# Another order of issue for a gated delta-rule kernel with a dense layer behind it

## The chip, the cores and the metric

The kernel runs on one core of one Trainium2 chip. The metric is the device time of one execution in microseconds, the median over runs. Engines are named as in the profile: PE is TensorE (matmuls; PEld its weight loads), DVE is VectorE, ACT is ScalarE, POOL is GpSimd, SP is SyncE, which here only issues DMAs.

## The reference

A gated delta-rule attention over 4 batches, 8 heads, 768 steps and a head size of 48, then a dense layer with softplus on its 3072 rows of 384:

```python
for t in range(S):                       # _attn_ref
    kt, vt, bt = k_n[:, :, t], v[:, :, t], beta[:, :, t, None]
    readout = einsum('bhd,bhde->bhe', q[:, :, t], state)
    y[:, :, t] = g[:, :, t] * readout
    v_old = einsum('bhde,bhd->bhe', state, kt)
    state = state + bt * einsum('bhd,bhe->bhde', kt, vt - v_old)
...
h = x @ w_in                             # _moe_ref: 384 -> 2048 -> 384
return (softplus(h) @ w_out).astype(float32)
```

`k_n` is k divided by its norm. Step t reads the state that the steps before it wrote.

## The kernel before

The 768 steps are cut into 12 chunks of 64 (`c`), worked on in pairs (`cc`). All 32 batch-heads of a chunk go together. Within a chunk the recurrence is solved as a triangular system, so that the state passes only from chunk to chunk. The work is a list of 1168 *steps*, each with a number, a kind, the engines that it may run on and the steps that it depends on. These functions add them:

- `load`, `load_q`: DMAs of k, q, v and g, one chunk in two halves, issued by SP (two of k by ACT); the weights `w_in` and `w_out` come in quarters, issued by POOL.
- `norms` and `front`, for a chunk: squares and sums of k (ksq, red), the root (pow on POOL, L541), k times its inverse norm (kmul, L303), transposes (trs, L321 and L364) and their copies (kev), and the gram matrices (L405, L406, L438, L475, L476) with their copies (kkc) and masks.
- `inverse`, for a pair of chunks: prep (L592) and 15 serial steps of two small operations (L602, L609) on POOL, for the first pair on DVE; then the matmul steps xmm (L665), tmm (L686, L692) and zmm (L718, L721).
- `chain`, for a chunk, the recurrence: ks and qs (L759), w (L793), umm (L802, L806), zu (L827), smm (L847), s (L862), ymm (L877), y (L892), and the transposes ytr (L911).
- `dense`, for one or two chunks: g1 (L941, h = x @ w_in, three matmuls 512 wide or six 256 wide a step), softplus on ACT (L953), g2 (L968, o = ga @ w_out, four matmuls 384 wide a step), the copy of o and the store.

A g1 or g2 step is few large matmuls on the whole array. The steps of `inverse`, `chain` and the gram matrices are 16 to 68 matmuls on parts of 32 to 64 rows. Every matmul has its own weight load, so that TensorE runs 6112 of each, 12,232 instructions with a few of the frame, with no loop: the program is one straight list.

Nothing plans at run time. The order is a table, `_ORDER` (L1022), of words such as `P665`: a letter for the engine (P TensorE, D DVE, A ACT, G POOL, S SP) and the number of the step. `Program.emit` goes through it once:

```python
for word in table.split():
    en, no = word[0], int(word[1:])
    it = self.items[no]
    ...
    for b in it.bufs:
        if b.ap is None:
            b.slot = b.ring.free.pop(0)
    it.fn(en)
```

The words of one engine, taken out of the table, are the order in which that engine works, and it works strictly in that order. A step that needs what another engine made waits on a semaphore. Buffers come from rings (4 of k, 3 of q, 4 of v, 3 of g, 5 PSUM banks `d` for the small work, 2 `h`, 1 `o`); the table also decides who gets which slot and so which step must wait until a slot is free.

Of the kernel before, what the change touches and what calls it, by code (L numbers as in the profile page):

```python
# [1019 lines left out]


_ORDER = """  # L1022
S0 D226 D152 A1 D111 P114 D110 P112 D115 P124 A9 G227 A104 D105 A113 P121 S8 A106 D131 P134 S26
S3 S27 A130 S19 P132 A135 P144 D107 S18 A123 A108 D126 A125 D133 P141 D109 A145 A146 D150 D153
S25 G212 A122 S17 S2 S10 S33 G196 P197 S11 S42 S16 S41 D142 A143 D151 S5 D154 D155 D156 D157
D158 D159 D160 D161 D162 D163 A198 S24 S7 A116 A117 P118 A119 S34 A120 P127 S32 S35 S43 S4 D164
D165 D166 D167 D168 D169 D170 G171 S13 D129 A187 A137 D172 A136 S40 P213 P138 D188 A547 G173
D174 A140 A139 P147 D148 A189 D190 S12 S6 D548 D549 P175 A177 P176 A178 A259 D260 D128 P179 A181
A554 P180 A182 D298 G96 A261 D262 G97 P183 A184 P555 A556 D214 G98 G191 D192 P550 A551 D193 P557
P552 A558 P565 A553 P563 G99 D566 D564 D284 P194 A195 S14 S15 G209 P567 D568 P569 D570 P210 A211  # L1030
D149 P832 A833 P559 D571 P560 D562 P199 A200 A202 D203 D201 P838 A839 D561 P215 A216 D217 P220
A223 A221 P836 A837 D222 G263 D224 D264 P204 A207 A205 D206 P834 A835 G100 D219 D218 P285 G101
G268 P269 A270 P840 D225 P572 P579 D573 P844 A286 A845 D580 G102 G265 P266 D267 P575 A576 D208
P185 A186 P582 D583 P271 A272 D273 P574 P581 P584 D585 P577 A841 A274 P846 D275 G281 P282 P592
D593 A578 P590 A283 P848 D591 P287 D291 D289 A847 G228 G229 G230 G103 P292 D296 D295 D288 D290
P594 A595 S49 P842 A843 P849 G231 P868 A869 G232 G233 D293 G234 G235 G236 G237 G238 G239 G240
G241 S51 P866 A867 P276 D277 D279 D280 D297 P587 P586 D588 D278 P870 A871 D589 G242 G243 G244
G245 D246 P860 A861 P850 P851 A852 P862 A863 D247 P864 A865 S48 A331 P854 P855 P856 P857 A858
S20 S57 P249 P250 A251 D248 P596 P598 P603 D332 D294 S56 A333 D334 P253 P252 P876 P877 A254 S21
D604 D597 P255 S50 P606 A607 P599 P257 P605 D256 P608 A600 P601 A602 G299 G300 G301 G302 G303  # L1040
S23 S29 D340 D609 P872 A873 P611 P610 D612 D613 P614 G335 A258 P874 A875 D336 P341 A342 P627 S28
D628 P620 S58 D621 G304 G353 S22 D615 P878 P879 A880 P623 D624 P630 A631 P616 D617 P629 P622
P625 D626 P632 A633 P354 A355 P638 S31 S30 D639 P640 D641 P635 P634 D636 D637 S59 A356 P882 P618
G337 P338 D339 P642 D643 P357 G305 G306 G307 G308 P883 G309 S64 S65 A403 D404 P348 D350 A619
P898 P890 A358 P364 D367 D366 S67 A349 G310 D352 D368 A351 S66 G412 P359 D361 D363 D362 A899
A891 S73 S72 A405 P918 A919 P900 A901 G311 G312 G313 G314 D406 G315 G316 D317 D318 P884 P902
A903 P892 A893 D319 P885 A365 A360 P910 A911 P908 A909 D320 P343 A346 S90 A344 D369 S881 G370
G371 D345 P321 P322 A323 S74 P896 A897 D886 P888 A889 P325 P324 D326 S37 P651 S36 D652 P644 D645
P646 D347 S81 S80 A475 D476 S83 P894 A895 P912 A913 P413 A414 P906 S39 P329 D330 A907 S75 P647
G372 G373 A648 G374 G375 P327 D328 P654 P916 A917 P904 D655 A905 D428 P653 P656 A657 P649 G407  # L1050
D408 S44 G409 D650 G376 S89 S88 S46 S82 A484 S887 S53 A477 G377 P429 P914 A915 G378 G379 P658
S38 S47 P659 S853 P920 G380 P921 D430 P922 D661 P923 P664 A924 D478 D660 P675 D665 S45 P668 S69
P926 P927 P928 P929 D669 D676 P678 D930 S931 A679 G381 P671 D672 G425 P662 D663 P677 P680 S61
A681 G479 P670 S62 S54 P673 A674 P932 G382 G383 G384 G385 G386 P666 D667 P426 D427 P933 P410
A411 P686 D687 P688 P934 P935 A936 G387 D689 P690 D691 S70 P420 D422 P415 A416 A418 S63 D419
P938 D417 D421 P960 A961 P966 A967 D423 P436 P431 D439 D435 A432 A434 D437 G388 D441 P948 A949
P958 A959 S60 P939 P950 D514 D438 A951 S52 D389 D433 S68 D390 S859 S91 P964 A965 D480 G391 D392
P940 P968 S77 A969 D424 G442 P962 A963 P682 G443 G444 P683 D684 G445 S55 G446 D685 P393 P394
A395 P944 A945 P952 A953 P396 P397 A398 P692 D693 P699 P954 A955 A500 P946 A947 P941 A942 S943
D700 P399 P702 P695 D400 A696 D703 P970 A971 P974 G447 S937 G448 G449 G450 G451 G452 G453 G454  # L1060
G455 A975 G456 G457 G458 G459 G460 P701 P704 P694 P697 D705 G497 P956 A957 P972 A973 D698 D440
D461 D462 D463 D464 P976 P977 P978 P979 A980 P707 P706 D708 D709 P712 D713 P982 P983 P984 P985
A986 S987 P723 D724 P710 P716 D717 P401 A402 P465 P726 D727 P719 A720 S981 D711 P466 A467 P725
P728 A729 P718 P721 D481 S93 S78 P714 D715 P988 A722 S71 P734 D735 P736 D737 P730 P731 D732 P482
S79 S85 P989 S95 A483 P485 D486 P738 D733 P498 D499 P990 P991 A739 D992 S993 P1004 A1005 P501
D502 P1028 A1029 P1022 P994 A1023 P503 A504 S84 D507 D505 P492 D493 D494 D496 A506 D495 P1012
A1013 P995 P1018 A1019 S94 P1008 A1009 P508 D512 A509 A511 P487 D491 D489 A488 A490 D513 P469
P468 A470 P1020 D510 A1021 P996 P1010 P740 P747 A1011 D741 P471 G515 G516 G517 G518 G519 G520
S76 A472 D748 P473 A474 P743 P750 D751 A744 P1006 A1007 P1000 A1001 G521 G522 G523 P749 P742
P752 A753 P745 A746 P997 D998 P1002 A1003 P1026 A1027 S999 P760 D761 P758 D759 P754 P755 D756  # L1070
P1024 A1025 S87 G524 G525 S86 P1016 A1017 D757 P762 D763 P1014 A1015 P1030 A1031 P1032 P1033
P1034 P1035 D1036 G526 G527 G528 G529 G530 G531 P771 G532 A533 D534 S925 D772 P764 P773 D765
P1038 P1039 P1040 P1041 D1042 S1043 P767 D768 P774 P538 A775 P766 P769 D770 P776 A777 P537 D539
P782 D783 P784 P778 P779 P1044 P1045 D785 P786 D787 P1046 P1047 A1048 S1049 P1058 A1059 P1076
A1077 P1050 P1060 A1061 P1070 A1071 G535 D536 P540 S92 P541 A542 D781 D780 P788 P795 P1068 P1062
D796 A1063 A1069 P1051 P1052 P1078 A1079 P1064 A1065 P798 A799 D789 P543 A544 P791 P1080 A1081
P1072 A1073 D792 P790 P793 A794 P797 P800 A801 P1086 A1087 P806 P802 P808 P803 P1056 D807 D805
P1053 A1057 D809 D804 P1082 A1083 P810 P1066 D1054 A1067 P1074 A1075 D811 P1088 S1037 S1055
P1084 P1089 P1090 A1085 P1091 A1092 P1124 A1125 P1118 A1119 P1100 P1101 P1102 P1103 P819 D1104
S1105 D820 P812 D813 P821 P1094 P1095 P1096 P1097 P1126 D1098 S1099 P822 A823 P545 P815 A546  # L1080
P1106 D816 A1127 P1112 A1113 P1107 P1114 A1115 P1108 P1109 A1110 P824 D825 P814 P817 A818 P1116
A1117 P1122 A1123 P828 P826 P1128 D829 P1120 D827 A1121 P830 P1129 P1130 S1093 P1131 A1132 S1133
D831 P1148 A1149 S1111 P1144 A1145 P1134 P1135 P1146 A1147 P1140 A1141 P1136 P1142 A1143 P1150
A1151 P1137 D1138 S1139 P1154 P1152 A1155 A1153 P1162 P1163 P1164 P1165 A1166 S1167 P1156 P1157
P1158 P1159 A1160 S1161
"""

# [28 lines left out]
```

## Time and profile before

| | us |
|---|---|
| median of 3 runs | 302.21 |
| lowest and highest | 299.0, 303.22 |
| the profiled execution | 303.66 |
| its span, first to last instruction | 301.7 |

The profile is of one execution. "Busy" of an engine counts its instructions; that of PE is modelled from starts. A wait is written `who <- whom`; "issue" stands for a wait with no cause in the records. Kinds of DMA queues: hardware_dynamic and software_dynamic carry data, "instruction" carries the engines' programs. PEclk is the granted clock of TensorE in tenths, or as a share of 1. The mean granted clock of this execution is 0.920.

### The profile page before, as it was taken

The page shows a single profiled execution, that of the slowest core. Times are in us where ns is not written, and L with a number is a line of the kernel's source. Part 1 is how long each engine was busy: PE and PEld are TensorE (multiplying, and loading weights), DVE is VectorE, ACT ScalarE, POOL GpSimd, SP SyncE. Part 2 cuts the span into 40 slices and gives each one's busy share as a digit, 9 for nine tenths or more (in the row PEclk, how much of TensorE's full clock was granted, in tenths as well). Part 3 has the DMA queues.
Part 4 walks back from the last instruction along what each step waited for, and adds up shares of the span by engine and source line. Part 5 has one row for each costly group of instructions (what it writes and reads, how often), then busy time and mean ns, then how long its engine had stood idle before and what let it go on. Part 6 is the DMA issues. An engine that isn't in the chain of part 4 may idle for free.

```text
span 301.7 us, 13385 instructions
## 1 busy us (share of the span) xinstructions
PE 236.7 (78%) x6112; PEld 161.7 (54%) x6112; DVE 141.0 (47%) x307; ACT 131.7 (44%) x239; POOL 119.7 (40%) x217
## 2 busy tenths in 40 slices
PE   1353239869949976989996996998996999999960
PEld 1233137656737833566653566764564556667730
DVE  7689447824824775374680453553433324112000
ACT  3546245743524764562463523265520355334510
POOL 7204809986361882749868500006820000000000
PEclk9999999977978999799997897798997899999995
DMA  8999998999501099530683012841031110011111
GB/s 126 201 179 186 186 182 141 191 202 161 109 4 30 25 168 163 128 83 8 129 148 69 13 43 65 140 93 31 20 88 32 33 50 9 22 45 39 39 50 42
DMA packets 85480, 27.69 MB, mean 92 GB/s; under 512 B 75568, under 2 KB 85424, under 8 KB 85424
## 3 DMA queue, kind: packets, MB, share of 16 engines
q1 hardware_dynamic: 79376, 23.21, 42.2%
q0 software_dynamic: 3968, 3.25, 7.0%
q8 instruction: 47, 0.77, 1.2%
q10 hardware_dynamic: 2080, 0.39, 0.9%
q14 instruction: 9, 0.07, 0.1%
HBM read 25.26 MB, written 4.72 MB: 99 GB/s over the span
## 4 chain that ended last, share of the span: by engine, by line
PE 70%; DMA 10%; issue 9%; SPq 2%; POOL 2%; ACT 2%; DVE 1%; POOLq 0%; ACTq 0%; DVEq 0%
PE h L941 23%; PE o L968 22%; DMA kf<-in_k_dram 5%; PE d L759 4%; DMA beta_l<-in_beta_dram 3%; PE d L877 2%; PE d L827 2%; DMA out_dram<-osb 2%; PE d L665 2%; PE d L847 2%; PE d L692 2%; PE d L321 2%; PE d L911 2%; PE d L475 2%; PE d L721 1%
## 5 line engine op out<-in xcount | busy, mean ns | idle before, releaser
L941 PE MATMUL h<-xt,w_in 128*128 128x512 f16 (+1 forms) x384 | 78.2, 344 | 1.9 <-ACT ga L953 1.9
L968 PE MATMUL o<-w_out,ga 128*128 128x384 f16 x384 | 75.1, 341 | 0.7 <-ACT osb L200 0.6
L953 ACT ACTIVATE ga<-h 128x512 f16<-128x512 f32 x96 | 57.0, 597 | 37.4 <-PE h L941 35.0
L968 PEld LDWEIGHTS <-ga 128*128 128x128 f16 x384 | 37.6, 102 | 26.6 <-issue 4.6
L941 PEld LDWEIGHTS <-w_in 128*128 128x128 f16 x384 | 36.4, 101 | 24.6 <-issue 5.4
L609 POOL TENSOR_TENSOR tt<-tt,tmp 128x30 f32<-128x30 f32 (+7 forms) x75 | 27.7, 369 | 5.9
L541 POOL TENSOR_TENSOR nv<-nv,half_c 128x32 f32<-128x32 f32 x5 | 27.2, 5449 | 6.6 <-DVE nv L524 6.6
L602 POOL TENSOR_TENSOR tmp<-nn,tt 128x30 f32<-128x30 f32 (+7 forms) x75 | 26.5, 353 | 5.4
L200 ACT ACTIVATE u<-d 128x384 f16<-128x384 f32 x30 | 14.3, 490 | 26.3 <-PE d L806 14.6
L592 POOL TENSOR_TENSOR nn<-ln,beta_l 128x256 f32<-128x256 f16 x10 | 6.0, 619 | 42.9 <-DVE ln L574 42.9
L200 ACT ACTIVATE kqt<-d 128x1024 f16<-128x1024 f16 (+1 forms) x18 | 15.5, 877 | 16.2 <-PE d L321 12.2
L303 POOL TENSOR_TENSOR kn<-kf,nv 128x768 f16<-128x768 f32 x8 | 12.5, 1573 | 19.6 <-DVE nv L547 14.5
L200 ACT ACTIVATE osb<-o 128x384 f32<-128x384 f32 x14 | 6.9, 490 | 29.6 <-PE o L968 24.7
L493 DVE TENSOR_TENSOR mt<-d,mask 128x256 f16<-128x256 f32 x40 | 15.4, 411 | 8.8 <-ACT kk L200 5.4
L892 DVE TENSOR_TENSOR yg<-d,gf 128x384 f16<-128x384 f32 x24 | 12.7, 552 | 14.2 <-PE d L877 14.2
L202 DVE COPY osb<-o 128x384 f32<-128x384 f32 x10 | 5.5, 554 | 28.2 <-PE o L968 28.2
L793 DVE TENSOR_TENSOR w<-vf,d 128x384 f16<-128x384 f32 x22 | 11.1, 547 | 15.4 <-PE d L759 15.4
L759 PE MATMUL d<-s,kqt 48*64 48x48 f16 x704 | 16.2, 195 | 2.1 <-issue 2.1
L665 PE MATMUL d<-tn,kk 16*32 16x16 f16 x768 | 8.6, 171 | 11.8 <-issue 10.6
L202 DVE CAST u<-d 128x384 f16<-128x384 f32 x18 | 9.9, 554 | 16.4 <-PE d L806 8.9
L759 PEld LDWEIGHTS <-kqt 48*64 48x64 f16 x704 | 13.4, 115 | 6.3 <-issue 5.9
L524 DVE TENSOR_REDUCE nv<-ksq 128x16 f32<-128x768 f32 x12 | 11.3, 942 | 10.1 <-ACT ksq L520 10.1
(104 smaller groups left out, 361.7 us busy)
## 6 DMA issues: line engine op xcount, KB each, us to landing
qf<-in_q_dram SPq DMA_DIRECT2D x24, 192.0 KB
vf<-in_v_dram SPq DMA_DIRECT2D x24, 192.0 KB
gf<-in_g_dram SPq DMA_DIRECT2D x24, 192.0 KB
out_dram<-osb SPq DMA_DIRECT2D x24, 192.0 KB
kf<-in_k_dram SPq DMA_DIRECT2D x22, 192.0 KB
w_in<-in_moe_w_in_dram POOLq DMA_DIRECT2D x4, 384.0 KB, 9.0
w_out<-in_moe_w_out_dram POOLq DMA_DIRECT2D x4, 384.0 KB, 8.4
kf<-in_k_dram ACTq DMA_DIRECT2D x2, 192.0 KB
```

What stands on the lines that cost most here:

```text
L200: nc.scalar.activation(o, x, AF.Copy, scale=float(sign))
L202: ENG[en].tensor_copy(o, x)
L493: nc.vector.tensor_tensor(mt[c][m].ap[:, NP * p : NP * p + NP], gb[m].ap.rearrange("p (n b) -> p n b", n=NP)[:, :, C:], mask[:, None, :].b ...
L541: lambda en: nc.gpsimd.tensor_tensor(nv.ap, nv.ap, half_c, ALU.pow),
L602: eng.tensor_tensor(t, nn.ap[:, :, j + 1 :, j : j + 1].broadcast_to([P, 2, n, w]), tt.ap[:, :, j : j + 1, :w].broadcast_to([P, 2, n, w]), ...
L609: eng.tensor_tensor(rows, rows, t, ALU.add)
L665: nc.tensor.matmul(uv(xp.ap)[QUAD[qd], u], kk.ap[r, 0, u, :], tn.ap[r, u, :])
L759: nc.tensor.matmul(hd(o.ap)[HALF[r], NP * p + i], kq_of(c)[FEAT[m], 8 * p + 2 * i + r, off : off + C], s0[r].ap[FEAT[m], NP * p + i], **st ...
L892: lambda en, m=m: nc.vector.tensor_tensor(heads(yg.ap, m), hd(yp[m].ap), heads(gf.ap, m), ALU.mult),
L941: nc.tensor.matmul(hp.ap[:, n * b : n * b + n], w_in[:, j, f * P : (f + 1) * P], xt.ap[:, j, t0 : t0 + n], start=(j == 0), stop=(j == 2),)
L953: lambda en, hp=hp, o=gb: nc.scalar.activation(o.ap, hp.ap, AF.Softplus),
L968: nc.tensor.matmul(op.ap[:, :DM], b.ap[:, col + c0 : col + c0 + 128], w_out[:, f, :], start=(f == 0), stop=(f == NF - 1),)
```

## The change

Only the table `_ORDER` is another one. The steps, their matmuls, their tiles, the rings, and everything outside the table are unchanged. Its author searched the order with a model in which TensorE fetches its instructions in lines of 256. The two tables have the same 1168 numbers; 105 of them carry another engine letter (kinds kkc, u1, o, kev, xt, kmul, u2, xs, z and some others), all among D, A and G. Of the 431 words for TensorE, 23 stand at the same place among TensorE's words as before. The start, a middle piece and the end:

```diff
 _ORDER = """
-S0 D226 D152 A1 D111 P114 D110 P112 D115 P124 A9 G227 A104 D105 A113 P121 S8 A106 D131 P134 S26
-S3 S27 A130 S19 P132 A135 P144 D107 S18 A123 A108 D126 A125 D133 P141 D109 A145 A146 D150 D153
+D226 S0 D152 A1 D111 D110 P114 P112 A9 A104 A115 P124 D105 S8 A130 D113 P121 D131 P134 A106 D125
+D126 P132 A133 P141 D107 A108 D109 D150 A135 P144 S18 A123 A122 A142 A145 D153 S11 A137 D143
...
-A223 A221 P836 A837 D222 G263 D224 D264 P204 A207 A205 D206 P834 A835 G100 D219 D218 P285 G101
-G268 P269 A270 P840 D225 P572 P579 D573 P844 A286 A845 D580 G102 G265 P266 D267 P575 A576 D208
-P185 A186 P582 D583 P271 A272 D273 P574 P581 P584 D585 P577 A841 A274 P846 D275 G281 P282 P592
+D264 D281 P215 D217 S14 A216 P220 A223 D224 D222 P579 D580 A218 A221 D225 S15 S35 S34 P842 A843
+D219 P285 A286 P572 D573 P582 D583 P282 A283 P834 P147 D149 A839 P575 A576 P581 P584 D585 A835
+G99 P846 A847 P574 P577 A578 D148 G100 D265 P592 D593 P844 P590 A845 D591 P287 A288 G102 S49
...
-A1151 P1137 D1138 S1139 P1154 P1152 A1155 A1153 P1162 P1163 P1164 P1165 A1166 S1167 P1156 P1157
-P1158 P1159 A1160 S1161
+P1140 A1141 P1137 D1138 S1139 P1146 A1147 P1150 A1151 P1156 P1157 P1158 P1159 A1160 S1161 P1162
+P1163 P1164 P1165 A1166 S1167
 """
```

Numbers under 96 are loads, 96 to 103 the weights, 104 to 546 `norms`, `front` and `inverse`, 548 to 831 `chain` and 832 to 1167 `dense`. In the old table stretches of P words with numbers under 832 alternate with stretches of P words from 832 up; in the new one both kinds alternate more often.

More of the change, by code (lines that the diff above doesn't have):

```diff
@@ L1022 @@
 _ORDER = """
-S0 D226 D152 A1 D111 P114 D110 P112 D115 P124 A9 G227 A104 D105 A113 P121 S8 A106 D131 P134 S26
-S3 S27 A130 S19 P132 A135 P144 D107 S18 A123 A108 D126 A125 D133 P141 D109 A145 A146 D150 D153
[L1025 to L1028, printed above, removed]
@@ L1029 @@
-A554 P180 A182 D298 G96 A261 D262 G97 P183 A184 P555 A556 D214 G98 G191 D192 P550 A551 D193 P557
-P552 A558 P565 A553 P563 G99 D566 D564 D284 P194 A195 S14 S15 G209 P567 D568 P569 D570 P210 A211
-D149 P832 A833 P559 D571 P560 D562 P199 A200 A202 D203 D201 P838 A839 D561 P215 A216 D217 P220
-A223 A221 P836 A837 D222 G263 D224 D264 P204 A207 A205 D206 P834 A835 G100 D219 D218 P285 G101
-G268 P269 A270 P840 D225 P572 P579 D573 P844 A286 A845 D580 G102 G265 P266 D267 P575 A576 D208
-P185 A186 P582 D583 P271 A272 D273 P574 P581 P584 D585 P577 A841 A274 P846 D275 G281 P282 P592
@@ L1035 @@
[L1035 to L1082, printed above, removed]
@@ L1083 @@
-D831 P1148 A1149 S1111 P1144 A1145 P1134 P1135 P1146 A1147 P1140 A1141 P1136 P1142 A1143 P1150
-A1151 P1137 D1138 S1139 P1154 P1152 A1155 A1153 P1162 P1163 P1164 P1165 A1166 S1167 P1156 P1157
-P1158 P1159 A1160 S1161
+D226 S0 D152 A1 D111 D110 P114 P112 A9 A104 A115 P124 D105 S8 A130 D113 P121 D131 P134 A106 D125
+D126 P132 A133 P141 D107 A108 D109 D150 A135 P144 S18 A123 A122 A142 A145 D153 S11 A137 D143
+D146 D151 D154 D155 D156 D157 D158 D159 D160 S25 D161 D162 A547 D163 D164 S12 D165 D166 D167
@@ new lines @@
+D168 S17 S3 A117 S2 A116 P118 A119 A120 P127 D169 D170 D171 G173 S16 A187 D172 P175 D188 A177
+D174 P179 S24 S19 S10 S4 A189 S5 D548 P176 A549 D554 A181 D190 D129 S13 P550 S40 S33 P183 D128
+S32 A259 D260 A136 A551 P555 D556 A184 P552 D178 D571 S6 S41 A261 S7 P557 G97 A553 P563 D564
+A558 P565 G98 G196 P197 D566 P569 G191 D192 D570 P567 A568 D262 D193 P138 D140 S26 D139 A198
+P180 P840 P194 S27 D195 A182 S42 S43 D284 A841 P185 A212 P836 A186 P204 D206 D208 A837 G96 A205
+P560 A207 P559 D561 D562 G209 P213 A214 P199 D203 D201 A202 P210 A211 P838 P832 A200 A833 G263
@@ new lines @@
+D264 D281 P215 D217 S14 A216 P220 A223 D224 D222 P579 D580 A218 A221 D225 S15 S35 S34 P842 A843
+D219 P285 A286 P572 D573 P582 D583 P282 A283 P834 P147 D149 A839 P575 A576 P581 P584 D585 A835
+G99 P846 A847 P574 P577 A578 D148 G100 D265 P592 D593 P844 P590 A845 D591 P287 A288 G102 S49
+A290 G227 P292 P594 A293 G268 S48 D291 D294 D595 A295 P848 A331 P266 P586 P587 D588 D267 D589
+P860 A861 P870 A871 P269 A270 P862 A863 G101 P866 A867 D289 P276 A279 G103 P271 A272 G228 A274
+D332 G229 G230 G231 G232 G233 G234 G235 G236 G237 G238 G239 G240 G241 D296 G242 P864 G243 D277
@@ new lines @@
+S57 D275 A865 D280 G244 D245 G247 P849 P850 P851 D246 P250 P249 P874 A852 D297 D278 S56 P854
+A333 D273 A251 D334 A875 G298 G299 G300 G301 D248 P868 P872 A869 A873 S65 S50 P253 P252 A254
+P855 G302 G303 P856 P857 P603 S64 A403 D404 S20 P596 A858 S21 P876 D604 P606 G335 P255 D597 P599
+A600 P877 P878 A607 D256 S75 S51 P598 P601 A602 D340 D336 D353 P605 P608 A609 G304 G305 P879
+A880 P610 P611 D612 D613 P616 S58 P614 P354 A355 P882 P257 A258 S28 S59 D356 S22 P341 P357 G306
+S23 D617 D615 P618 A342 G307 A358 P622 D337 P627 P620 P883 S72 S29 D619 D628 P630 D621 P359 P623
@@ new lines @@
+D631 D361 S73 A405 D406 D363 S74 P884 A624 S31 A360 P625 G308 G309 S30 A362 G310 G311 P629 P632
+A633 G312 G313 G314 G315 G316 D317 D318 S81 P885 P640 D641 A626 P638 D639 P338 D339 G428 P429
+A430 P635 P634 D637 D636 P642 A643 P343 D345 G319 A344 P348 D351 D346 D352 A349 P902 A903 S68
+P364 A365 D366 D367 S80 D369 P888 A889 P908 A909 D368 G407 D408 D347 P322 D442 A475 P894 A895
+P904 A905 P321 A323 D476 P651 P644 P916 A917 D320 P910 A911 G370 G425 P426 S36 P896 P325 A897
+S45 S89 S88 A477 S37 D645 D652 D427 P324 A326 P912 A913 P906 D478 A907 P431 D433 S853 P890 A891
@@ new lines @@
+P918 A919 P647 D350 D435 D434 P654 A655 P327 A328 P900 A901 P898 A899 P646 S66 S39 D648 P649
+D650 P892 S44 S67 A412 P914 A893 D432 P653 P656 A657 P662 D886 G371 S881 S38 D663 P329 A915 D330
+P658 P659 D661 D660 P664 D665 G372 D409 P413 A414 P920 P921 P922 P923 D924 P436 A437 A439 D438
+D440 P675 G373 D676 G374 P668 D669 P926 S859 S82 G375 P927 S52 G479 D480 P410 S887 A411 P666
+D667 G376 G377 P678 A679 P671 G378 G379 G380 G381 S83 D672 P928 P929 S84 S71 D930 P677 P680 A681
+P670 P673 A674 S53 S46 P938 P939 S47 P686 D687 P688 D689 P940 P941 G382 D942 G383 G384 P690 A691
@@ new lines @@
+P420 A421 D423 P415 A416 D417 S91 G385 G386 G387 G388 G389 D390 G443 G391 P932 S70 D422 P933
+P958 A959 P948 A949 D418 D441 P393 D419 P394 D395 P683 P682 D685 P946 A947 P954 A955 G497 P934
+P966 A967 D392 P962 D514 G515 A963 S90 A500 P498 P970 P974 A975 D684 D481 P699 P692 P397 P396
+D484 A971 D700 D693 D398 P964 A965 P944 S925 S931 P501 A945 A502 D424 P956 A957 P399 A400 P401
+S55 P702 A703 D499 G444 G445 G446 G447 G448 G449 G450 G451 G452 G453 G454 G455 G456 G457 G458
+G459 G460 P695 D696 S63 D402 P935 D936 P968 A969 P694 P697 D698 P701 P704 S76 D705 P972 A973
@@ new lines @@
+P485 G461 A486 P710 S54 D711 P712 D713 P707 P706 D708 S943 P952 A953 S85 P482 D483 P714 A715
+P950 A951 S60 P960 A961 P503 A504 P492 D496 A493 A495 D709 D494 S87 S937 D506 D505 S61 P982 P983
+P984 P985 D986 P508 A511 P723 D724 A509 P716 P988 P989 D512 D717 P990 S69 P991 P487 A490 A488
+D462 D507 S93 D992 P726 S993 P719 D513 P976 P977 A727 P978 P979 D510 A463 D489 P725 A720 P718
+P728 D980 P721 A722 P994 D729 P736 P731 P734 P730 S62 S92 P995 P996 S981 S987 D737 D735 P738
+D739 P466 P465 P1010 P1002 P997 G516 A1011 A1003 P1022 A1023 S86 S77 P1012 A1013 D467 D464 P469
@@ new lines @@
+D998 P1028 A1029 G517 G518 G519 G520 G521 G522 G523 G524 G525 S78 P1016 A1017 P468 A470 G526
+P1024 A1025 P1000 A1001 D733 D732 P749 P747 P740 D741 D491 D748 P1014 G527 A1015 P1030 A1031
+G528 G529 G530 G531 G532 D533 D534 P471 D472 P743 A744 P750 D751 P1004 A1005 P1006 P742 A1007
+P745 D746 P752 A753 P1008 A1009 P1026 A1027 P473 P538 D474 P1020 A1021 P1018 P754 P755 D756 D757
+A1019 P1038 P1039 P1040 P1041 P760 P758 D1042 P764 D761 S79 P771 D772 D759 P1032 P1033 P1034 S94
+P1035 A1036 P774 D765 P767 A768 D775 P537 D539 D535 P766 P773 P776 P769 D770 D777 D536 P762 A763
@@ new lines @@
+S999 P1050 P1051 P1052 P1053 P779 P784 P778 D780 D785 P782 A1054 D783 S1043 P1044 P1045 P1046
+P786 D787 P540 D781 P541 D542 P1060 A1061 P1056 P788 A1057 D789 P795 D796 P1078 A1079 P1070
+P1047 A1071 A1048 P1076 A1077 P1082 A1083 P543 P798 D799 A544 P791 D792 P1058 A1059 P797 P800
+D801 P790 P793 D794 P1064 A1065 P1084 A1085 S95 P808 D809 P802 P803 D804 P806 D805 D807 P1062
+A1063 P1086 A1087 S1037 P819 S1049 P821 D820 P812 S1055 D813 P1072 P1066 A1073 A1067 P810 D811
+P1068 A1069 P1088 P1074 A1075 P1080 P1089 P1090 A1081 P1091 D1092 P1126 A1127 P1124 A1125 P1094
@@ new lines @@
+P1095 P1096 P1097 A1098 P815 A816 P822 D823 P545 A546 S1099 P1100 P1101 P1102 P1103 D1104 P824
+D825 P814 P817 A818 P1106 P828 D829 P826 P1118 A1119 P1112 A1113 S1093 P1107 P1122 A1123 D827
+P830 D831 P1114 A1115 P1116 A1117 S1105 P1108 P1109 D1110 S1111 P1154 P1120 P1128 A1155 P1129
+A1121 P1130 P1131 P1152 A1132 A1153 P1142 A1143 P1134 P1135 S1133 P1148 A1149 P1136 P1144 A1145
+P1140 A1141 P1137 D1138 S1139 P1146 A1147 P1150 A1151 P1156 P1157 P1158 P1159 A1160 S1161 P1162
+P1163 P1164 P1165 A1166 S1167
```

## The prediction

> **What bounds the kernel now.** I begin with the page: busy shares, slices, DMA queues, chain of waits.
>
> ```profile
> span 301.7 us, 13385 instructions
> PE 236.7 (78%) x6112; PEld 161.7 (54%) x6112; DVE 141.0 (47%) x307; ACT 131.7 (44%) x239; POOL 119.7 (40%) x217
> ...
> PE   1353239869949976989996996998996999999960
> ...
> PEclk9999999977978999799997897798997899999995
> ...
> q8 instruction: 47, 0.77, 1.2%
> ...
> PE 70%; DMA 10%; issue 9%; SPq 2%; POOL 2%; ACT 2%; DVE 1%; POOLq 0%; ACTq 0%; DVEq 0%
> ```
>
> TensorE is 78% busy and carries 70% of the chain; no other engine is above 47%. The next share but one is "issue", 9%, or 27 us: the engine stood still and waited for nothing that the profile shows. The dips in the PE row and in the row of its clock come in pairs. So the question is what stops TensorE. The table of its waits from 74.85 us to the end (total, times, longest) says:
>
> ```profile
> PE d L665 <- issue: 7.3, 3, 2.6
> PE d L692 <- issue: 2.8, 3, 2.1
> PE d L759 <- issue: 2.1, 1, 2.1
> PE d L847 <- issue: 2.0, 1, 2.0
> PE h L941 <- ACT ga L953: 1.9, 1, 1.9
> PE d L827 <- issue: 1.4, 2, 0.8
> PE d L806 <- issue: 1.4, 1, 1.4
> PE o L968 <- ACT osb L200: 0.6, 1, 0.6
> ```
>
> "issue" is 7.3+2.8+2.1+2.0+1.4+1.4 = 17.0 us; all other waits are 1.9+0.6 = 2.5 us. Every one stands before a line of tiny matmuls, and inside a step, not at its start, so no semaphore explains it. The timeline of TensorE around two of them shows why:
>
> ```profile
> 83.25 0.78 PE L759 MATMUL d<-s,kqt 48*64 48x48 f16 x43
> 86.11 0.25 PE L759 MATMUL d<-s,kqt 48*64 48x48 f16 x5 [2.08 <-issue]
> 86.29 0.36 PE L686 MATMUL d<-td,ident 32*32 32x256 f16 x4
> 86.43 0.70 PE L692 MATMUL d<-td,xs 32*16 32x16 f16 x64
> 86.96 0.41 PE L686 MATMUL d<-td,ident 32*32 32x256 f16 x4
> 87.14 0.59 PE L692 MATMUL d<-td,xs 32*16 32x16 f16 x51
> 89.84 0.24 PE L692 MATMUL d<-td,xs 32*16 32x16 f16 x13 [2.11 <-issue]
> ```
>
> From the one stop to the next are 5+4+64+4+51 = 128 matmuls, each with its weight load: exactly 256 instructions. Counting all records of TensorE from the start, the 15 such stops of over half a microsecond stand behind instructions 706, 962, 1218, 1986 and so on, all 194 + 256n. The page has the other half: 47 transfers of kind "instruction" on q8 with 0.77 MB, 16 KB each, and 12,232 instructions in blocks of 256 make 47.8. So TensorE's program arrives in blocks of 256, one ahead, and a block run through faster than the next arrives ends in a stop. The price is in the same rows: 89.84 - 86.11 = 3.73 us from block to block, however little is in it.
>
> [...]
>
> **What the change does.** It only permutes the table of steps: 1168 words before and after, 6112 matmuls and 6112 weight loads in both. 105 steps change engine, all copies, casts, clears and multiplies of DVE, ACT and POOL; the largest is kmul, of which five go from POOL to DVE. I cut TensorE's instructions of both orders at 194 + 256n and priced each block from these pieces of the chain:
>
> ```profile
> 65.44 0.73 PE d L321 x8
> ...
> 155.22 1.29 PE h L941 x6
> 156.51 0.52 PE d L847 x31
> 157.03 1.09 PE d L665 x123
> 158.12 2.44 issue
> ...
> 165.64 2.67 PE h L941 x6
> ...
> 173.79 2.60 PE o L968 x16
> ...
> 282.63 1.31 PE h L941 x12
> ```
>
> A 512-wide L941 is 1.29/6 = 0.215 us, a 256-wide one 1.31/12 = 0.109, an L968 2.60/16 = 0.163, a transpose 0.73/8 = 0.09, a small matmul between 1.09/123 = 0.009 and 0.52/31 = 0.017; I take 0.0115, near the many. I number the blocks so that block 9 is entered at 74.85 us.
>
> Before, from block 9 on, eight blocks (10, 11, 17, 25, 30, 35, 38, 39) hold no L941 or L968 at all and cost 128 x 0.0115 = 1.5 us of the 3.73; a dozen more lie between 2.5 and 3.4. What all blocks lack to 3.7 us is 26.6 us by this sum, of which 17.0 show as stops (the rest is covered by hand-overs inside the steps, and some blocks come sooner).
>
> After, from block 9 on, no block is without L941 or L968. The poorest are 16 (2.8 us), 21 and 26 (3.2), 11, 12, 13, 36 and 42 (3.3); the sum to 3.7 us is 4.1. Scaled as before, 4.1 x 17.0/26.6 = 2.6, I leave 3 us of stops: **-14 us**. Bounds: -17 (none left) and, if the stop per block is 4.1 us and nothing is covered, about -9.
>
> Blocks 1 to 8 don't gain. Here the stop takes longer:
>
> ```profile
> 26.72:74.85 48.13, 30.16 (x1039) 24.35 (x1034) 26.67 (x52) 21.48 (x41) 35.86 (x50) 0.93 1.14 180
> 74.85:291.60 216.75, 197.07 (x4892) 130.60 (x4868) 92.69 (x182) 96.06 (x172) 75.47 (x146) 0.92 0.32 65
> ```
>
> ```profile
> 32.75 0.29 PE L665 MATMUL d<-tn,kk 16*32 16x16 f16 x17 [3.27 <-issue]
> 39.22 0.27 PE L692 MATMUL d<-td,xs 32*16 32x16 f16 x17 [4.01 <-issue]
> ```
>
> The first fence has two stretches (length, busy time of PE, weight loads, DVE, ACT and POOL, clock, DMA share, GB/s), the second the timeline. With the DMA full (180 GB/s), a block takes 39.22 - 32.75 = 6.47 us; eight took 48.13, and 30 us of work (29.9 before, 30.4 after by the prices) lies under that floor in both orders, with the same loads ahead of it on SP (32 by block 8 in each). I take 0, bounds -5 to +5.
>
> The second term is the clock. The stretches of half clock in 74.85 to 291.60 are six, 34.1 us; the first and last of them for L968, and the sums for L968 and then for L941:
>
> ```profile
> 86.38:93.21 6.83, 2.74 (x8) 1.01 (x8) 0.50 0.02 5
> ...
> 229.74:236.57 6.83, 4.28 (x13) 1.91 (x14) 0.50 0.05 19
> sum 34.14, PE 9.26 PEld 4.20; mean PE 1.54 PEld 0.70
> ```
>
> ```profile
> sum 34.14, PE 9.24 PEld 2.20; mean PE 1.54 PEld 0.37
> ```
>
> At half clock six L941 take 2.67 us, at full clock 1.29; so of 9.26 + 9.24 us half, 9.2 us, is lost. Each stretch begins in or shortly behind a stop (158.12, then half clock and 2.67 at 165.64). With the stops spread, I expect one or two stretches left: **-7.5 us**, bounds 0 and -9. [...]
>
> The third term is cover. The 17.0 us of stops were time in which ACT, DVE and POOL caught up; without them the 2.5 us of other waits may grow. DVE and ACT have 92.7 and 96.1 us of work in 216.75, under half even of 195, so the five kmul more of DVE are hidden there. POOL's inverses are the long serial part:
>
> ```profile
> 205.58 1.20 POOL L592 TENSOR_TENSOR nn<-ln,beta_l 128x256 f32<-128x256 f16 x2 [34.47 <-DVE ln L574]
> ```
>
> POOL waited 34.47 us for the last one; so it has room. Between the last gram step and the first xmm step of the pairs 1 to 5 lie, by the block sums, 22, 30, 33, 36 and 23 us after, against 26, 43, 41, 30 and 25 before. The two short ones could be late by about 3 us each. On SP's queue the shortest lead of a load, from when its buffer is free to its first user, falls from about 24 us to 7 (g of chunk 7, behind four other loads). I take **+1.5 us** for all of this, bounds 0 and +12.
>
> **The sum.** This execution took 303.66 us, 1.96 of it around the span, and 1.45 above the median of 302.21. 303.66 - 14 - 7.5 + 1.5 = 283.7; less 1.45 gives **282 us**.
>
> **Rivals.** *No change, 296 to 305.* The transfers on q8 are a symptom and the stops stay, or the freed time is simply waited for elsewhere. [...] Were only half of the stops gone and the clock as before, it would be 302.2 - 8.5 = 294, so more must fail than that: about 15 us of new waits on top of the forecast. Against it: stops exactly 256 apart, and 2.5 us of other waits in 217. For it: xmm leads of 22 and 23 us. Chance 0.11.
>
> *Slower, 325.* The stop grows instead of going: after issues work sooner, so the loads of chunks 4 to 11 fall together, and a fetch behind a full DMA takes 6.2 us as it did up to 74.85 us. Blocks 9 to 28 after hold about 4.0 us each; at 6.2 that is 20 x 2.2 = 44 us, 282 + 44 = 326. It decides against the change from about 5.4 us per block (20 x 1.4 = 28). Against it stands the burst at 116 us, where the DMA was as full:
>
> ```profile
> 116.18:117.46 1.28, 1.28 (x136) 1.11 (x136) 0.02 (x1) 1.18 (x4) 0.00 (x0) 1.00 1.48 176
> ```
>
> ```profile
> 120.19 0.32 PE L665 MATMUL d<-tn,kk 16*32 16x16 f16 x25 [2.56 <-issue]
> ```
>
> That block took 120.19 - 116.18 = 4.0 us, not 6.2. Chance 0.05.
>
> *The stops go, the clock doesn't.* The term of 7.5 falls away: 290. It is inside the range.
>
> **How the numbers follow.** A measurement here can tell about 2%, 6 us, from no change. The forecast, faster to under 296.2, has 0.84, no change 0.11, slower 0.05. Low end: all stops and the whole clock term gone, no new waits, and 5 us off blocks 1 to 8: 303.7 - 17 - 9.2 - 5 - 1.45 = 271, rounded to 270. High end: -9 of stops, -7.5 of clock, +12 of waits is 298; I put 297, so that the no-change case is touched, and slower left out.
>
> **What will show it.** The waits of TensorE from block 9 on should have about 3 us of "issue" in place of 17.0, no stop over 1.5 us there; before it eight blocks should still take about 48 us; q8 still 47 transfers. Half clock after the first 75 us in at most two stretches; pieces of 2.67 us for six L941 rare. The block edges should come 3.6 to 4.0 us apart in the middle. It is wrong if stops remain at block edges that hold L941 and L968, or if TensorE waits over 10 us for ACT, DVE, POOL or loads.

## The result and the profile after

| | before | after |
|---|---|---|
| median, us | 302.72 (4 runs) | 282.25 (4 runs, 278.84 to 283.57) |
| ratio to before | | 0.929 [0.910, 0.948] |
| profiled execution, its span | 303.66, 301.7 | 283.57, 281.6 |

The change is worth 20 us, the 282 us of the forecast. Ratios to before, here and below, compare the faster executions of both kernels, with a 95% interval. The page of the new kernel:

```profile
span 281.6 us, 13376 instructions
PE 231.0 (82%) x6112; PEld 156.3 (56%) x6112; DVE 147.9 (53%) x316; ACT 129.7 (46%) x234; POOL 117.4 (42%) x213
...
PE   1322379876989997999999998699999999999960
...
PEclk9999999997979999999999999959999999999995
...
q8 instruction: 47, 0.77, 1.2%
...
PE 56%; DMA 12%; DVE 12%; issue 7%; POOL 7%; ACT 2%; SPq 1%; DVEq 0%; ACTq 0%; POOLq 0%
```

The same 47 transfers bring the program, but from the 13th slice to the 38th only the 16th and the 26th of the PE row are under 8 tenths, and of the clock row only the 27th is under 9. Block 9 is entered at 73.38 us. The waits of TensorE from there on (total, times, longest), all of them:

```profile
PE d L911 <- DVE yg L892: 2.8, 2, 2.3
PE d L475 <- issue: 1.6, 1, 1.6
PE d L665 <- issue: 1.1, 1, 1.1
PE o L968 <- ACT osb L200: 0.8, 2, 0.6
PE d L476 <- issue: 0.5, 1, 0.5
PE d L802 <- DVE mt L493: 0.4, 1, 0.4
PE d L475 <- DVE w L793: 0.3, 1, 0.3
PE d L721 <- issue: 0.2, 1, 0.2
PE d L475 <- DVE s L862: 0.2, 1, 0.2
```

"issue" is 1.6+1.1+0.5+0.2 = 3.4 us in place of 17.0; the others are 4.5 in place of 2.5. Half clock comes in two stretches, 10.25 us together, with these sums, first for L941, then for L968:

```profile
sum 10.25, PE 6.51 PEld 3.15; mean PE 3.26 PEld 1.57
...
sum 10.25, PE 2.27 PEld 0.69; mean PE 1.14 PEld 0.35
```

Half of 6.51 + 2.27 is 4.4 us lost, in place of 9.2. So an account can be made for every run: from the entry of block 9 to the last matmul, the issue waits, the other waits, half the busy time of L941 and L968 at half clock, and the rest.

| run | profiled, us | block 9 to end | issue | other waits | half clock | rest |
|---|---|---|---|---|---|---|
| before | 303.66 | 217.0 | 17.0 | 2.5 | 9.2 | 188.3 |
| after | 283.57 | 199.0 | 3.4 | 4.5 | 4.4 | 186.7 |
| before, L968 spread | 302.01 | 214.2 | 8.5 | 11.2 | 6.1 | 188.4 |
| after, L968 clustered | 311.68 | 226.2 | 4.0 | 19.2 | 8.5 | 194.5 |
| after, old letters | 300.29 | 217.6 | 3.1 | 19.8 | 4.8 | 189.9 |
| after, five kmul on POOL | 290.16 | 207.0 | 4.0 | 9.5 | 5.3 | 188.2 |
| after, old letters but kmul | 303.18 | 216.7 | 3.2 | 15.0 | 8.2 | 190.3 |
| before, new letters | 335.25 | 239.9 | 12.9 | 14.0 | 20.9 | 192.1 |
| before, edges 64 on | 298.69 | 210.7 | 10.8 | 2.5 | 8.2 | 189.2 |
| after, edges 96 on | 284.02 | 204.1 | 6.4 | 3.5 | 3.5 | 190.7 |
| after again | 282.44 | 196.4 | 2.3 | 3.6 | 3.8 | 186.7 |
| after, two loads earlier | 276.05 | 190.2 | 1.6 | 1.1 | 1.0 | 186.5 |

The rest is 186 to 192 us in all runs but one (194.5): mostly TensorE's own work, which is the same in every order, with waits too short to be listed and whatever half clock costs the small matmuls. Most of what differs is in the three columns ahead of it; differences of a few us are lost in the rest. The profiled execution is one of several, and of two kernels one of the longest (303.18 against a median of 297.28 for the old letters but kmul, 335.25 against 330.18 for the old order with the new letters), so the columns say what kind of wait leads, and tenths in them mean nothing.

### The profile page after: what moved, and what is told of

Its sections match the earlier page's. It is cut to its first block, busy times and chain, and to the rows that moved or that the text cites. A ratio compares the mean times of both kernels' runs of the same rounds, so it can differ in the third digit from the quotient of the medians.

```text
span 281.6 us, 13376 instructions
## 1 busy us (share of the span) xinstructions
PE 231.0 (82%) x6112; PEld 156.3 (56%) x6112; DVE 147.9 (53%) x316; ACT 129.7 (46%) x234; POOL 117.4 (42%) x213
## 4 chain that ended last, share of the span: by engine, by line
PE 56%; DMA 12%; DVE 12%; issue 7%; POOL 7%; ACT 2%; SPq 1%; DVEq 0%; ACTq 0%; POOLq 0%
PE h L941 20%; PE o L968 15%; DMA gf<-in_g_dram 4%; DMA vf<-in_v_dram 3%; PE d L759 3%; DMA out_dram<-osb 2%; DMA beta_l<-in_beta_dram 2%; PE d L364 2%; POOL nv L541 2%; PE d L827 2%; POOL tmp L602 2%; PE d L692 2%; POOL tt L609 1%; PE d L877 1%; PE d L475 1%
## 5 line engine op out<-in xcount | busy, mean ns | idle before, releaser
L941 PE MATMUL h<-xt,w_in 128*128 128x512 f16 (+1 forms) x384 | 76.8, 341 | 2.1 <-issue 2.1
L968 PE MATMUL o<-w_out,ga 128*128 128x384 f16 x384 | 71.3, 332 | 1.0 <-ACT osb L200 0.8
L968 PEld LDWEIGHTS <-ga 128*128 128x128 f16 x384 | 36.2, 99 | 23.5 <-issue 2.2
L941 PEld LDWEIGHTS <-w_in 128*128 128x128 f16 x384 | 35.8, 102 | 24.0 <-issue 5.1
L609 POOL TENSOR_TENSOR tt<-tt,tmp 128x30 f32<-128x30 f32 (+7 forms) x75 | 30.4, 406 | 5.9
L202 DVE COPY osb<-o 128x384 f32<-128x384 f32 x14 | 7.8, 554 | 25.2 <-PE o L968 25.2
L202 DVE CAST u<-d 128x384 f16<-128x384 f32 x22 | 11.9, 554 | 17.1 <-PE d L806 10.3
L200 ACT ACTIVATE kqt<-d 128x1024 f16<-128x1024 f16 (+1 forms) x19 | 17.0, 908 | 7.9 <-PE d L364 4.4
L200 ACT ACTIVATE u<-d 128x384 f16<-128x384 f32 x26 | 12.4, 490 | 15.4 <-PE d L827 11.5
L200 ACT ACTIVATE kk<-d 128x256 f16<-128x256 f32 x35 | 11.9, 386 | 13.9 <-PE d L476 11.7
L827 PE MATMUL d<-u,z 64*64 64x48 f16 x384 | 11.3, 191 | 6.2 <-issue 5.8
L321 PE MATMUL d<-ident,kn 128*128 128x128 f16 x96 | 9.1, 251 | 7.1 <-DVE kn L202 7.1
L665 PE MATMUL d<-tn,kk 16*32 16x16 f16 x768 | 8.2, 172 | 7.7 <-DVE tn L627 5.1
```

The lines of the kernel that those rows point to most:

```text
L200: nc.scalar.activation(o, x, AF.Copy, scale=float(sign))
L202: ENG[en].tensor_copy(o, x)
L609: eng.tensor_tensor(rows, rows, t, ALU.add)
L827: nc.tensor.matmul(hd(vp.ap)[HALF[r], pi], z.ap[HALF[r], 2 * pi + m, :], u1.ap[HALF[r], pi],)
L941: nc.tensor.matmul(hp.ap[:, n * b : n * b + n], w_in[:, j, f * P : (f + 1) * P], xt.ap[:, j, t0 : t0 + n], start=(j == 0), stop=(j == 2),)
L968: nc.tensor.matmul(op.ap[:, :DM], b.ap[:, col + c0 : col + c0 + 128], w_out[:, f, :], start=(f == 0), stop=(f == NF - 1),)
```

## The experiments

**Are the stops a matter of place in the program?** Small matmuls ahead of everything, in idle time, move every edge of a block against the work. For the old kernel 32 (64 instructions), for the new one 48:

```diff
+    for i in range(32):
+        qd = i % 4
+        r = slice(32 * qd, 32 * qd + 16)
+        nc.tensor.matmul(p_o.tiles[0][QUAD[qd], :16], ident[r, :32], ident[r, :16])
     prog.emit(_ORDER)
```

> The old kernel with 32 small matmuls and their weight loads ahead of everything: block edges move 64 instructions. Block theory: every stop moves by 32 matmuls, and the sum falls from 26.7 to 21.0, so issue waits after block 9 fall from 17.0 to about 13.5 us: 297 to 302 us. Rival (stops belong to steps): the same matmuls stop, 17 us, 302 to 305 us.

298.69 us, ratio 0.989 [0.983, 0.995]. Two lines of the timeline of TensorE:

```profile
89.81 0.47 PE L692 MATMUL d<-td,xs 32*16 32x16 f16 x45 [2.23 <-issue]
...
198.82 0.28 PE L692 MATMUL d<-td,xs 32*16 32x16 f16 x19 [2.47 <-issue]
```

In the old kernel the first of these steps stopped with 13 matmuls of L692 left; now 45 are left: the stop has moved by 32 matmuls, as the edge did. The second stop is new: the old kernel has none between 186 and 207 us. All issue stops of over 0.4 us stand at the new edges. Issue waits are 10.8 us, 2.7 less than expected. The stops belong to the program's blocks and not to any step.

> The new kernel with 48 small matmuls and their weight loads ahead of everything, in the time in which TensorE has nothing to do: every block edge moves 96 instructions towards the front of the work, nothing else changes. What the blocks lack to 3.7 us rises from 4.3 to 14.3 by the sum. Block theory: issue waits after block 9 rise from 3.4 to about 10 us, 286 to 292 us. Rival (stops belong to certain steps, or the place of the edges doesn't matter): 280 to 284 us.

283.94 us, ratio 0.941 [0.936, 0.946], which can't be told from the new kernel; issue waits are 6.4 us. They rose by 3.0, not by 6.6, and the time is in the range of the rival in which the place of the edges doesn't matter. Yet with these edges two blocks, 19 and 25, hold no large matmul. Block 19 took 2.5 us and ended in a stop of 1.1; block 25 is, but for a matmul or two, the second line here, and TensorE runs straight through it:

```profile
142.82 1.24 PE L941 MATMUL h<-xt,w_in 128*128 128x512 f16 x5
143.99 1.17 PE L665 MATMUL d<-tn,kk 16*32 16x16 f16 x128
145.09 0.59 PE L847 MATMUL d<-u,kn 64*64 64x48 f16 x32
```

The 16 KB transfer on q8 here began at 142.50 us, 1.5 us before TensorE entered block 25; in the old kernel those at blocks 10 to 12 began 1.0 to 1.2 us after the entry. So a transfer can begin ahead of the edge, and an empty block does not stop TensorE by itself. What lets it begin early isn't shown; the sum by blocks, which counts only what a block holds, can't see it and mostly makes the stops too large.

**What does a block cost by itself?** Behind the last L968, 2048 matmuls of 16x16, and from their eighth block on 24 loads:

```diff
     prog.emit(_ORDER)
+    for i in range(16 * 128):
+        qd = i % 4
+        r = slice(32 * qd, 32 * qd + 16)
+        x = mask if i < 7 * 128 else ident
+        nc.tensor.matmul(p_o.tiles[0][QUAD[qd], :16], ident[r, :32], x[r, :16])
+    nc.sync.dma_start(out=mask.bitcast(F32), in_=moe_w_in[:128, :32])
+    for i in range(24):
+        nc.sync.dma_start(
+            out=r_k.tiles[i % 4][64 * (i // 4 % 2) : 64 * (i // 4 % 2) + 64].rearrange("t p h d -> t (p h) d"),
+            in_=k[0:2, :, 64 * (i % 12) : 64 * (i % 12) + 64].rearrange("p h t d -> t (p h) d"),
+        )
```

> The new kernel with 16 blocks (2048 matmuls of 16x16 with their weight loads) behind its last L968, where no engine has other work; from the eighth on, SP issues 24 loads of 192 KB. Block theory: 128 such matmuls take 1.2 to 1.5 us, and a block still takes 3.7 us without loads; with the loads 4 us by the row at 116 us of the old kernel, or 6.2 us as before 74 us. Rival (TensorE can run straight on): 1.2 to 1.5 us a block.

The timeline of TensorE in the tail:

```profile
277.66 1.19 PE L1024 MATMUL o<-mask,ident 16*32 16x16 f16 x128 [2.53 <-issue]
281.39 1.20 PE L1024 MATMUL o<-mask,ident 16*32 16x16 f16 x128 [2.54 <-issue]
284.85 1.20 PE L1024 MATMUL o<-mask,ident 16*32 16x16 f16 x128 [2.25 <-issue]
...
300.34 1.20 PE L1024 MATMUL o<-ident 16*32 16x16 f16 x128 [3.25 <-issue]
304.89 1.34 PE L1024 MATMUL o<-ident 16*32 16x16 f16 x128 [3.36 <-issue]
309.72 1.19 PE L1024 MATMUL o<-ident 16*32 16x16 f16 x128 [3.49 <-issue]
```

No other engine computes, and TensorE stops after every 128 matmuls. A block is 1.2 us of work and takes 281.39 - 277.66 = 3.73, then 3.46 us; with the loads 304.89 - 300.34 = 4.55 and 4.83. The floor of the prediction, 3.73 us, is confirmed by itself, and loads raise it by about a quarter. That the transfers are no mere symptom shows in the old kernel's trace: each of its 15 stops ends 1.2 to 1.7 us after the end of a 16 KB transfer on q8.

**Why do blocks take over 6 us at the start?** The new kernel without the eight weight loads:

```diff
-                    lambda en, dst=dst, src=src: nc.gpsimd.dma_start(out=dst, in_=src))
+                    lambda en, dst=dst, src=src: nc.gpsimd.memset(dst[:1, :1, :1], 0.0))
...
+    nc.gpsimd.memset(w_in, 0.01)
+    nc.gpsimd.memset(w_out, 0.01)
```

> The new kernel without the eight loads of the weights, which POOL issues on q0 (w_in and w_out are filled with 0.01 instead, so the dense layer computes with other weights). Theory: it is the load of the DMA engines that makes a block before 74 us take about 6.2 us; with 3.1 MB of some 13 MB less in that time, blocks 2 to 8 take under 5.5 us. Rival (the number of transfers of 192 bytes, or the wait for what SP loads, sets it): still 6 us and over.

One stretch, 45 to 74 us, in the new kernel and then in this one (columns as in the prediction):

```profile
45.00:74.00 29.00, 23.16 (x644) 18.09 (x641) 17.37 (x35) 16.90 (x32) 20.62 (x44) 0.94 1.20 179
```

```profile
45.00:74.00 29.00, 26.74 (x843) 21.45 (x842) 22.67 (x44) 21.55 (x43) 21.35 (x51) 1.00 0.89 152
```

644 matmuls in 29 us are 29 x 128 / 644 = 5.8 us a block, 843 are 4.4. The window holds other blocks in the two runs, but from edge to edge it is the same: blocks 2 to 7 took 66.21 - 29.73 = 36.48 us in the new kernel and 60.81 - 34.60 = 26.21 here, 6.1 and 4.4 us a block, and the issue waits of blocks 1 to 8 fell from 11.7 to 2.4 us. With so few stops left, 4.4 us is mostly work, and the floor lies under it. So the load of the DMA (its share is 1.20, and 0.89 without the weights) makes the floor of 6 us, and without the weights it is gone; whether it is their bytes or their own queue isn't shown. What the load delays is the start of a transfer: in the old kernel the 16 KB took 0.9 to 1.7 us throughout, but began up to 4.3 us behind the edges of blocks 1 to 8, over 2.6 us at six of the eight; in the tail they began 1.0 to 1.4 us behind the edge without loads, 1.1 to 2.2 with them. The run took 275.16 us (one run), though its first blocks come 5 to 6 us later, behind the filling of the two tiles.

**Is spreading the large matmuls enough?** In the old order only words of g2 (L968), with the copy and the store behind them, are moved, 45 words; the first of the moves:

```diff
-P860 A861 P850 P851 A852 P862 A863 D247 P864 A865 S48 A331 P854 P855 P856 P857 A858 S20 S57 P249 P250 A251 D248
+P860 A861 P862 A863 D247 P864 A865 S48 A331 S20 S57 P249 P250 A251 P850 P851 A852 P854 P855 P856 D248
```

> The old order, in which only steps of L968 (g2), with the copy and the store behind them, are moved, so that fewer of TensorE's blocks go without large matmuls: what the blocks lack to 3.7 us falls from 26.7 to 11.7 us by the sum, no letter and no other step is moved. Block theory: 15.0 x 17.0/26.6 = 9.6 us of stops go, and some 3 us of the half clock: about 290 us, issue waits after block 9 near 7.5 us. Rival (the gain came from the rest of the order: loads, POOL, ACT, DVE): 299 to 306 us.

301.89 us (296.47 to 302.68) against 304.33 (299.34 to 306.62) of the kernel before on the same chip: little or nothing. The stops went as expected, 17.0 to 8.5 us, but the gain did not come out. From the waits of TensorE from block 9 on:

```profile
PE d L802 <- DVE w L793: 2.7, 2, 2.1
PE o L968 <- ACT osb L200: 2.5, 3, 1.2
...
PE d L759 <- DVE s L862: 2.0, 3, 1.5
...
PE o L968 <- DVE osb L202: 1.6, 3, 0.6
```

Other waits rose from 2.5 to 11.2 us, as much as the stops fell. The one `o` bank is waited for where g2 groups now meet, and the chain's DVE steps come too late, it seems because TensorE no longer stops. The opposite edit on the new order, 55 words of g2 with copies and stores brought together (the first: `P849 P850 P851` behind `P250 P249 P874`):

> The new order, in which only L968 steps, with copy and store behind them, are moved, the other way: together, so that what the blocks lack to 3.7 us rises from 4.3 to 23.9 us. Block theory: 19.6 x 0.64 = 12.5 us more stops and some 4 us of half clock, 296 to 300 us. Rival (rest of the order): 280 to 286 us.

309.51 us, ratio to before 1.017 [1.009, 1.025], and 27 us over the new kernel, above both ranges. But the extra time is not where it was expected: though nine blocks from block 9 on now hold no large matmul, issue waits stay at 4.0 us, and other waits rise to 19.2:

```profile
PE d L911 <- DVE yg L892: 7.6, 3, 5.1
...
PE o L968 <- ACT osb L200: 1.7, 3, 0.6
PE o L968 <- DVE osb L202: 1.6, 3, 0.7
```

It seems that where TensorE waits for an engine the next block arrives meanwhile, so that the two kinds of wait cover each other. This is read from the two sums, 19.2 us of other waits beside 4.0 of stops; transfers that begin early can be part of it, and no run parts the two.

**What do the 105 letters do?** The new order with the old letters, and the old order with the new ones; a piece of the first:

```diff
-D105 S8 A130 D113 P121 D131 P134 A106 D125 D126 P132 A133
+D105 S8 A130 A113 P121 D131 P134 A106 A125 D126 P132 D133
```

> The new order with the engine letters of the old table (105 steps go back to their old engine). Block theory (what decides is how L941 and L968 are spread over TensorE's blocks of 256): TensorE's list is unchanged, so about 3 us of issue waits after block 9 stay; some new waits for the changed engines, 280 to 290 us. Rival, the letters (POOL relieved of five kmul, copies better shared out): most of the 20 us are lost, 295 to 303 us.

301.38 us, ratio 0.989 [0.982, 0.996]: nearly all of the gain is gone, and yet the issue waits after block 9 are 3.1 us. The largest waits from there on:

```profile
PE d L665 <- DVE tn L627: 4.1, 2, 3.4
PE d L877 <- DVE u L202: 2.3, 1, 2.3
PE d L911 <- DVE yg L892: 2.3, 2, 2.0
PE d L827 <- DVE u L202: 1.8, 1, 1.8
```

> The old order with the engine letters of the new table. Block theory: stops stand at the same instructions as before, 17 us of issue waits after block 9, 298 to 306 us. Rival, the letters: 283 to 292 us.

330.18 us (322.45 to 335.25), against 304.33 of the kernel before: slower than either theory has it, with 12.9 us of issue waits, 14.0 of other waits and 20.9 lost to half clock. The letters fit the new order and not the old one. To part them, first the five kmul alone back on POOL (`D281 D265 D353 D337 D409` become G):

> The new order and its letters, with only the five kmul (chunks 4 to 8) put back from DVE to POOL, 1.57 us each. Theory POOL: these five make the inverses late, and most of the 15 us of other waits of the run with all old letters come back, on L665 behind DVE tn: 290 to 298 us. Rival: the other 100 letters matter (copies between ACT and DVE): 281 to 287 us.

289.98 us, ratio 0.962 [0.954, 0.969], other waits 9.5 us. Of these only 2.0 stand where they were expected, at L665 behind DVE tn; the largest, 2.5, is L364 behind a cast of POOL. And the counterpart:

> The new order with the old letters, but the five kmul on DVE as in the new kernel: the counterpart of the run with only these five put back. If the two parts of the letters add, this is 7 to 10 us under the run with all old letters, 291 to 295 us, and the other waits after block 9 fall from 19.8 to 10 to 14 us, above all at L665. Rival (the copies' letters alone make it late): 298 to 303 us.

297.28 us, ratio 0.984 [0.980, 0.988], between the two ranges; other waits 15.0 us, and the waits at L665 no longer lead. Against the new kernel (0.929 to 0.936) the five kmul alone cost about 3% when they go back; without the other 100 letters they bring back half a per cent, which the intervals don't tell from nothing. The parts don't add. The other 100 letters, 88 of them between ACT and DVE, carry the larger part; which of them wasn't tried.

**The late load.** The chain of waits of the new kernel, around its one dip:

```profile
173.91 7.46 DMA gf<-in_g_dram
...
181.49 1.03 DVE yg L892 x2
...
182.57 0.82 PE d L911 x6
183.39 1.13 PE d L665 x113
184.52 2.67 PE h L941 x6
```

The load of g of chunk 7 is issued at 173.9 us, lands 7.5 us later, y and its transpose wait, and the clock halves at the end of the wait, at 182.44 us (2.67 us for six L941). On SP's queue it stands behind loads that wait for buffers, though its own buffer was there since the load of its other half. Two words are moved:

```diff
-P695 D696 S63 D402
+P695 D696 S63 S62 D402
...
-P950 A951 S60 P960
+P950 A951 S60 S61 P960
...
-D506 D505 S61 P982
+D506 D505 P982
...
-P734 P730 S62 S92
+P734 P730 S92
```

> The new kernel once more, beside the next one on the same chip: 279 to 285 us, again a wait of over 2 us of L911 for DVE and behind it one stretch of half clock near 182 us.

280.48 us, ratio 0.936 [0.929, 0.942]; the wait and the half clock are there again.

> The new kernel with two loads of SP moved forward, each right behind the load of the other half of its tile: S62 (g of chunk 7) and S61 (v of chunk 7). Theory: the wait at L911 (2.6 us between two matmuls) and the half clock behind it (4.4 us of loss after block 9 in all) come from this one late load; both go, 4 to 6 us under the new kernel, 275 to 279 us. Rival: TensorE then waits a little later for another engine, under 1.5 us gained.

275.84 us, ratio 0.922 [0.916, 0.928], 4.6 us under the new kernel beside it on the same chip: faster than both, its slowest run (277.33) under the fastest of that kernel (277.49). The waits of TensorE from block 9 on are now

```profile
PE d L476 <- issue: 1.0, 1, 1.0
PE o L968 <- ACT osb L200: 0.6, 1, 0.6
PE d L911 <- DVE yg L892: 0.3, 1, 0.3
```

and four of 0.2, and 1.0 us is lost to half clock in place of 3.8.

## Why the prediction was right

**Stops, -14 us.** 17.0 became 3.4, -13.6. The mechanism is shown: stops move with the edges of blocks, by 32 matmuls for 64 instructions, and a block alone costs 3.46 to 3.73 us, about what was read from one pair of stops. The size was partly luck: the same sum by blocks missed the issue waits of the four other orders and shifts that it was tried on by 1 to 12 us, in three of them too large; it sees neither transfers that begin early nor what other waits cover. Of the signs, the longest stop is 1.6 us where none over 1.5 was to be left, and the edges of blocks 9 to 30 came 3.2 to 7.4 us apart, not 3.6 to 4.0. Small stops did stay at edges of blocks that all hold L941 or L968; the longest stands behind block 16, the poorest of the forecast.

**Clock, -7.5 us.** 9.2 became 4.4, -4.8. Two stretches were left, the upper end of "one or two"; the longer one isn't a leftover of a stop but follows the late load. With that load moved, 1.0 us is left in place of the 3.8 of the run beside it.

**Other waits, +1.5 us.** 2.5 became 4.5, +2.0, and 2.3 of the 4.5 stand at the place that was named, the load of g of chunk 7. POOL's inverses weren't late: L665 waits for no engine after block 9.

**Blocks 1 to 8, 0.** Two stretches of the new kernel, from block 1 and from block 9 on, beside the two of the prediction:

```profile
25.60:73.38 47.78, 34.31 (x1041) 27.27 (x1035) 30.16 (x54) 25.24 (x47) 35.61 (x50) 0.96 1.16 186
73.38:271.92 198.54, 190.30 (x4883) 124.47 (x4883) 96.65 (x187) 92.61 (x166) 74.65 (x144) 0.97 0.35 71
```

47.78 us in place of 48.13. Block 1 is entered 1.1 us earlier, which wasn't foreseen.

**The sum.** -13.6 - 4.8 + 2.0 = -16.4 behind block 9; the rest of the work there is 1.6 us shorter, the entry of block 9 comes 1.5 us earlier and the tail is 0.6 shorter: -20.1, as 301.7 - 281.6. The clock term was some 3 us too large, and these small gains, which weren't forecast, made up for it; that the sum came out to the microsecond is luck.

**What it had not seen.** It put the 105 letters at nothing, since DVE and ACT are under half busy. In the new order they were worth nearly the whole gain: with the old ones the stops go just the same, and 19.8 us of other waits take their place. The busy share hid that TensorE, in strict order, waits for single steps of DVE and ACT. So the +1.5 us for other waits came true only because the letters had been chosen along with the order, which the forecast gave no reason for. The rival in which "the freed time is simply waited for elsewhere" is what happens to the order alone, and to spreading L968 alone; its chance of 0.11 was for the whole, in which order and letters fit. The other rival, slower by 44 us on blocks 9 to 28, fell: full loads make a block 4.3 to 4.8 us, not 6.2, in the tail.

## What to carry to other kernels

TensorE, with a straight program of 12,232 mostly tiny instructions, was here held up by the arrival of that program, in the old order for 17.0 us from block 9 on. In a kernel like it, look for waits on nothing inside a step, count the instructions between them (256 here), and see that the blocks hold enough work to last until the next has come (here 3.5 to 3.7 us with the DMA nearly idle, about 6 under the loads of the start); a sum by blocks shows where to look, not how large each stop will be. Taking the stops away paid only where the other engines kept up with the tighter order, so engine choices and order had to be found together: the order alone gave 1%, with 19.8 us of other waits, and the engine choices alone made the kernel slower, 330.18 us. Then look at what the queue of loads has put behind a load that isn't its own.

## What the runs showed of the hardware

From one edge of a block of 256 of TensorE's instructions to the next it took 3.5 to 3.7 us in the tail with the DMA nearly idle (share 0.02), mostly 4.3 to 4.8 under 24 loads (share 1.00, 151 GB/s), and about 6 at the start of the kernel: 6.0 over blocks 1 to 8 of the old kernel (180 GB/s), 6.1 over blocks 2 to 7 of the new one. Matmuls of 16x16 on four quadrants with their weight loads took 1.2 us for 128 pairs, 9 ns each, at half clock in the tail, and 1.17 at full clock at 82.15 us of the old kernel. In the tail, where small matmuls and stops took turns, the clock was full up to 273.37 us, where no gap of the tail had been over 2.1 us, and half from 277.66 us, with stops of 2.3 to 2.5 us between 1.2 us of matmuls (the column before the last two):

```profile
269.43:273.37 3.94, 2.40 (x255) 2.26 (x254) 0.00 (x0) 0.00 (x0) 0.00 (x0) 1.00 0.15 53
...
277.66:292.03 14.37, 4.79 (x513) 4.41 (x514) 0.00 (x0) 0.00 (x0) 0.00 (x0) 0.50 0.02 5
```
